# A train of 88 small matmuls at the head of TensorE's program, and all of group 0's first product in halves

## The chip, the cores and the metric

The kernel runs on one core of one Trainium2 chip. The metric is the device time of one launch in microseconds, the median of several executions. The profile is of one execution.

## What is computed

Two attentions over the same q, k and v (8 batches, 8 heads, 576 positions, 64 columns) are added, and the sum, laid out as 4608 tokens of 512 columns, goes through two matrix products with a gated activation between them. Cut to what matters:

```python
q_d, k_d, v_d = (t.reshape(B, H, S // 4, 4, D).mean(axis=3) for t in (q, k, v))
out_up = np.repeat(softmax(scale * q_d @ k_d.T) @ v_d, 4, axis=2)
scores = np.where(np.abs(pos[:, None] - pos[None, :]) < 4, scale * q @ k.T, -1e9)
x = (out_up + softmax(scores) @ v).transpose(0, 2, 1, 3).reshape(B * S, H * D)
h = x @ w_in                      # 4608x512 @ 512x2048
out = (h / (1 + np.exp(-1.702 * h))) @ w_out   # 4608x2048 @ 2048x512
```

## The kernel before

The tokens are cut into 9 groups of 512 (`TG`). For each group the first product (`mm1`, issued by `hps_mm`, L814) makes sixteen 128x512 accumulators, one for each chunk `ffc` of 128 hidden columns, each a sum over four chunks `dmc` of 128 model columns. ScalarE takes each through Silu into `gT` (L825). The second product (`mm2`, L892) multiplies `gT` by `w_out`. While group g is multiplied, the attention of batch g+1 is worked into the same TensorE program at hand-written positions (`POS`, `POS_0`), so that its output `xT` is there for the groups that follow.

The order on every engine is written by hand; nothing is scheduled. TensorE's program begins (L952 and on) with `warm(2)`: two matmuls of zeros in fp32, 128x128 by 128x512, each of which the hardware runs as two passes. They read `wz`, which VectorE's first instruction sets to zero (L126). Then come `bars0` (L411: the diagonal band of the score mask, from `id128` and `off`), a filler matmul of zeros (L959 in the profile), the scores of batch 0 (`scores0`, L423, which need `kT` and `qT`, the transposes of the first loads of k and q, L311), another `warm` on `PM[0]`, the coarse scores (`scores_d`, L466), the products with v (`av_local0`, L520; `av_down0`, L533), the pooled v (`prep_vd_pe`, L388), and four calls of `turned` (L575), which transpose the normalised result `y` (L557, VectorE) into PSUM; copies on ScalarE and VectorE (L586, L587) bring it to `xT`. Between the last `turned` calls stand the first parts of group 0's first product (`part`).

GpSimd issues the loads of k, q, v for batch 1 and of the weights, in one queue (q0 on the page): q and k of batch 0, v of batch 0, `w_in` in three parts (L281), k and q of batch 1 (L218), `w_out` in two parts (L290), the ten half chunks of v for batch 1 (`load_vb`, L249), and `w_out`'s other two parts. `prep_vd_pe(1, ...)` reads all five chunks of v for batch 1; it stands at place 36 of group 0 (`VDP_0`).

`hps_mm` issues one 512 column matmul, or two of 256 columns where `halved` holds. Before, that is in group 0 for `ffc` under 9 and `dmc` over 0, and in group 1 for `ffc` under 8 and `dmc` over 0. Each matmul in the program is a weight load (LDWEIGHTS, rows PEld) and a MATMUL (rows PE), so each halving adds two instructions to TensorE's program and no arithmetic.

Of the kernel before, what the change touches and what calls it, by code (L numbers as in the profile page):

```python
# [15 lines left out]
TG = 512  # L16
# [3 lines left out]
def kernel(  # L20
# [9 lines left out]
    nc = tc.nc  # L30
# [5 lines left out]
    n_dmc = d_model // 128  # L36
# [31 lines left out]
    for _ in range(2):  # L68
        t = work.tile([128, 2 * (S + SD)], FP32, name="l", tag="l", bufs=2).bitcast(BF16)
# [9 lines left out]
    def pm_tile():  # L79
        turn["m"] += 1  # L80
        return PM[turn["m"] % 2]

    wz = consts.tile([128, 512], BF16, name="wz")
# [92 lines left out]
    def make_up():  # L176
        nc.scalar.copy(out=up, in_=id128[:, :, None].to_broadcast([128, 128, 4]))
# [111 lines left out]
    def load_w_out(c):  # L289
        nc.gpsimd.dma_start(  # L290
            out=w_out_bf[:, 4 * c : 4 * c + 4, :],
            in_=bass.AP(
                tensor=moe_w_out.tensor, offset=moe_w_out.offset + c * 512 * d_model,
                ap=[[d_model, 128], [128 * d_model, 4], [1, d_model]],
            ),
        )
# [135 lines left out]
    def scores_mixed(b, qd, P):  # L432
        def local(i, a, half):
            for r in range(4):
                par = half if r < 2 else 1 - half
                rows = slice(32 * r, 32 * r + 32)
                k0 = 114 * i + KSTART[par]
                q0 = 114 * i + QSTART[par]
                nc.tensor.matmul(  # L439
                    P[1 + r // 2][64 * par : 64 * par + 64, r % 2, 60 * i : 60 * i + 60],  # L440
                    lhsT=kT[b, qd][rows, k0 : k0 + 64, a],
                    rhs=qT[b, qd][rows, q0 : q0 + 60, a],
                    start=(a == 0), stop=(a == 1),
                    tile_position=(32 * r, 64 * par),
                )

        if qd:
            for n in range(10):
                local(n // 2, n % 2, 0)
        for n in range(6):  # L450
            scores_d(b, qd, P[0], (n,))
            for a in range(2 if n < 5 else 0):
                local(n, a, 1)
        if not qd:
            for n in range(10):
                local(n // 2, n % 2, 0)
        return P[0], P[1:3]
# [17 lines left out]
    def exp_local(qd, sp, us=(0, 1)):  # L475
        for u in us:
            nc.scalar.activation(  # L477
                out=es[2 * qd + u][:, :, 0:300], in_=sp[u][:, :, 0:300],
                func=AF.Exp, scale=inv_sqrt_d,
            )  # L480
# [21 lines left out]
    def exp_down(qd, sd):  # L502
        nc.scalar.activation(  # L503
            out=eds[qd][:, :, 0:432], in_=sd[:, :, 0:432],
            func=AF.Exp, scale=inv_sqrt_d / 16.0,
        )

    def mask_local(qd):
        for u in range(2):
            ev = es[2 * qd + u][:, :, 0:300]  # L510
            nc.vector.tensor_tensor(out=ev, in0=ev, in1=mask, op=ALU.mult)  # L511
# [77 lines left out]
    def sub(t, off, *dims):  # L589
        return bass.AP(  # L590
            tensor=t.tensor, offset=t.offset + off,
            ap=[list(t.ap[0])] + [list(d) for d in dims],
        )
# [181 lines left out]
    def warm(n, t=None):  # L775
        t = pm_tile() if t is None else t
        for _ in range(n):
            nc.tensor.matmul(
                sub(t, 0, (256, 2), (1, 256)), lhsT=wzf[:, 0:128],
                rhs=wzf[:, None, :].to_broadcast([128, 2, 256]),  # L780
                start=True, stop=True,
            )

    def attention(b):
        st = {}

        def s_pe(qd):
            P = PB if b == 1 else PA
            st["d", qd], st["s", qd] = scores_mixed(b, qd, P)

        def s_act(qd):
            if qd == 0:
                nc.scalar.preload_act_table_set("natural_log_exp_and_others")
            if qd:
                exp_down(qd, st["d", qd])
            exp_local(qd, st["s", qd], (1, 0) if qd else (0, 1))
            if not qd:
                exp_down(qd, st["d", qd])
            mask_local(qd)

        def s1():
            s_pe(1)
            s_act(1)

        first = [lambda: s_pe(0), lambda: s_act(0), s1]
        if b == 1:
            return first + [lambda hp=hp: avx1(b, hp) for hp in range(HP)]
        return first + [lambda: avx(b, (0, 1)), lambda: avx(b, (2, 3))]

    def hps_mm(g, ffc, dmc, acc):  # L810
        halved = dmc and (ffc < 9 if g == 0 else g == 1 and ffc < 8)
        n = TG // 2 if halved else TG
        for c in range(0, TG, n):
            nc.tensor.matmul(  # L814
                acc[:, c : c + n],
                lhsT=w_in_bf[:, dmc, ffc * 128 : (ffc + 1) * 128],
                rhs=xT[dmc][:, g * TG + c : g * TG + c + n],
                start=(dmc == 0), stop=(dmc == n_dmc - 1 and c + n == TG),
            )

    def new_gT():
# [7 lines left out]
    def mm1(g, gT, steps):  # L829
        two = [PA[i][:, u, :] for i in range(3) for u in range(2)]  # L830
        bank, abreast = [PM[0], two[0], PM[1], two[2], two[4]], 4
        if g == 0:
            bank = acc[0:6] + late
        elif g == 1:
            bank, abreast = [two[0], two[2], two[1], two[3], PM[1]], 5
            bank = bank + [PM[0], two[4], two[0], two[2]] + PM[::-1] * 4
        else:
            bank = bank + bank + PM + PM + PM
        for ffc in range(n_ffc):
            for f in steps.get(ffc, ()):  # L840
                f()
            if g and ffc < abreast:
                if ffc == 0:
                    for dmcs in ((0, 1), (2,), (3,)):
                        for u in range(abreast):
                            for dmc in dmcs:
                                hps_mm(g, u, dmc, bank[u])
            elif g or ffc > 5:
                for dmc in range(n_dmc):
                    hps_mm(g, ffc, dmc, bank[ffc])  # L850
            else:
                continue
            silu(gT, ffc, bank[ffc])
# [94 lines left out]
    for qd in range(NQ):  # L948
        load_qk(1, qd)
    load_w_out(0)  # L950
    load_w_out(1)
    warm(2)  # L952
    make_up()
    make_psel0()
    prep_1("k", 0, 0)
# [5 lines left out]
        rhs=wzf[:, None, 0:196].to_broadcast([128, 2, 196]),  # L961
        start=False, stop=True, skip_group_check=True,
# [62 lines left out]
    def part(ffcs, *dmcs):  # L1025
        for dmc in dmcs:
            for ffc in ffcs:
                hps_mm(0, ffc, dmc, acc[ffc])
# [13 lines left out]
    for g in range(n_groups):  # L1042
# [36 lines left out]
        if b < B:  # L1079
            for n, f in zip(POS if g else POS_0, attention(b)):  # L1080
                steps.setdefault(n, []).append(f)
            if g == 0:
                steps.setdefault(VDP_0, []).append(lambda: prep_vd_pe(1, flat(PB[2])))
# [33 lines left out]
```

## Time and profile before

| | |
|---|---|
| median of 3 runs (lowest, highest) | 313.28 us (313.2, 314.6) |
| the profiled execution's own time | 313.27 us |
| its span, first to last instruction | 311.5 us |
| TensorE: matmul rows | 303.0 us busy, 4175 |
| TensorE: weight load rows | 157.4 us busy, 4175 |
| ScalarE, VectorE, GpSimd | 203.6, 147.6, 147.0 us busy |

The profiled execution's time is 1.8 us over its span, which is what lies around the first and the last instruction. Rows named PE are matmuls, PEld weight loads; a row of the timeline has start, length, engine, line, operation, what is written and read, the shape, a count, and in brackets the engine's idle time before it with what ended it ("issue" where the profile shows nothing that it waited for). Instruction loads have DMA queues of their own on the page (q8, q14).

### The profile page before, as it was taken

The page shows a single profiled execution, that of the slowest core. Times are in us where ns is not written, and L with a number is a line of the kernel's source. Part 1 is how long each engine was busy: PE and PEld are TensorE (multiplying, and loading weights), DVE is VectorE, ACT ScalarE, POOL GpSimd, SP SyncE. Part 2 cuts the span into 40 slices and gives each one's busy share as a digit, 9 for nine tenths or more (in the row PEclk, how much of TensorE's full clock was granted, in tenths as well). Part 3 has the DMA queues.
Part 4 walks back from the last instruction along what each step waited for, and adds up shares of the span by engine and source line. Part 5 has one row for each costly group of instructions (what it writes and reads, how often), then busy time and mean ns, then how long its engine had stood idle before and what let it go on. Part 6 is the DMA issues. An engine that isn't in the chain of part 4 may idle for free.

```text
span 311.5 us, 9625 instructions
## 1 busy us (share of the span) xinstructions
PE 303.0 (97%) x4175; PEld 157.4 (51%) x4175; DVE 147.6 (47%) x303; ACT 203.6 (65%) x325; POOL 147.0 (47%) x169
## 2 busy tenths in 40 slices
PE   7889999999999999999999999999999999999995
PEld 3557554664544554455545554555454544444444
DVE  5974937851594059605970399028902760000000
ACT  4746766787857786668866895689558857216611
POOL 8632294297039933795369634983396110000000
PEclk9999999999999999999999999999999999999999
DMA  6999999989727941695169705981520110010011
GB/s 103 162 211 207 170 105 210 229 236 184 192 99 162 216 124 69 170 230 145 69 165 204 176 36 175 194 189 58 151 75 33 39 67 2 34 67 36 0 67 67
DMA packets 64042, 39.94 MB, mean 128 GB/s; under 512 B 44544, under 2 KB 54912, under 8 KB 64000
## 3 DMA queue, kind: packets, MB, share of 16 engines
q0 software_dynamic: 18784, 14.95, 33.7%
q1 hardware_dynamic: 45072, 24.32, 28.4%
q8 instruction: 32, 0.52, 0.7%
q14 instruction: 10, 0.08, 0.1%
q10 hardware_dynamic: 144, 0.07, 0.1%
HBM read 44.83 MB, written 9.44 MB: 174 GB/s over the span
## 4 chain that ended last, share of the span: by engine, by line
PE 93%; DVE 2%; DMA 2%; issue 1%; ACT 1%; POOL 0%; DVEq 0%; ACTq 0%; POOLq 0%
PE pm L892 37%; PE pm L814 25%; PE pa L814 16%; PE pa L439 3%; PE pa L892 2%; PE pa L701 2%; PE pa L679 2%; PE pa L466 2%; DMA qb<-in_q_dram 2%; PE pm L909 1%; PE pa L575 1%; DVE qT L311 1%; PE pa L616 1%; PE pa L604 0%; PE pa L520 0%
## 5 line engine op out<-in xcount | busy, mean ns | idle before, releaser
L892 PE MATMUL pm<-w_out_bf,gT 128*128 128x512 bf16 x528 | 119.4, 379 | 0.0
L814 PEld LDWEIGHTS <-w_in_bf 128*128 128x128 bf16 x627 | 60.8, 98 | 61.5 <-issue 0.3
L814 PE MATMUL pm<-xT,w_in_bf 128*128 128x512 bf16 (+1 forms) x364 | 88.5, 372 | 0.0
L892 PEld LDWEIGHTS <-gT 128*128 128x128 bf16 x560 | 52.8, 98 | 62.4 <-issue 0.6
L825 ACT ACTIVATE gT<-pm 128x512 bf16<-128x512 f32 x88 | 52.8, 604 | 38.8 <-PE pm L814 38.8
L814 PE MATMUL pa<-xT,w_in_bf 128*128 128x512 bf16 (+1 forms) x263 | 59.0, 347 | 0.0
L511 DVE TENSOR_TENSOR es<-es,mask 128x600 bf16<-128x600 bf16 x28 | 17.3, 653 | 86.0 <-ACT es L477 85.8
L877 ACT ACTIVATE osb<-pm 128x512 f32<-128x512 f32 (+2 forms) x35 | 20.3, 582 | 30.5 <-PE pm L892 28.0
L825 ACT ACTIVATE gT<-pa 128x512 bf16<-128x512 f32 x56 | 31.8, 609 | 7.7 <-PE pa L814 7.7
L771 POOL TENSOR_TENSOR xT<-xT,od 128x576 bf16<-128x576 bf16 x12 | 15.4, 1282 | 43.7 <-DVE xT L755 43.7
L755 DVE TENSOR_TENSOR xT<-n,l 128x285 bf16<-128x285 f32 (+1 forms) x96 | 28.1, 363 | 0.0
L342 POOL TENSOR_TENSOR pq<-kT 128x576 f32<-128x576 bf16 x11 | 12.8, 1159 | 30.4 <-DVE kT L311 30.4
L879 DVE TENSOR_SCALAR osb<-pm 128x128 f32<-128x128 f32 x1 | 0.3, 292 | 53.8 <-ACT osb L877 53.8
L359 POOL TENSOR_TENSOR pq<-v 112x512 f32<-112x512 f32 x18 | 23.7, 1319 | 0.0
L311 DVE STREAM_TRANSPOSE kT<-kb 128x576 f32<-128x576 f32 x16 | 19.9, 1244 | 4.8 <-DMA kb<-in_k_dram 4.8
L311 DVE STREAM_TRANSPOSE qT<-qb 128x576 f32<-128x576 f32 x16 | 19.8, 1237 | 0.4 <-DMA qb<-in_q_dram 0.2
L503 ACT ACTIVATE ed<-pa 128x864 bf16<-128x864 f32 x16 | 14.3, 894 | 7.3 <-PE pa L466 7.3
L477 ACT ACTIVATE es<-pa 128x600 bf16<-128x600 f32 x28 | 17.2, 669 | 0.1
L750 ACT ACTIVATE l<-l 128x1440 f32<-128x1440 f32 x12 | 16.8, 1404 | 0.4
L745 DVE COPY n<-pa 128x492 f32<-128x492 f32 x24 | 15.0, 665 | 2.3 <-ACT l L744 1.7
L744 ACT ACTIVATE l<-pa 128x492 f32<-128x492 f32 x24 | 12.6, 578 | 4.2 <-PE pa L701 3.3
L439 PE MATMUL pa<-qT,kT 32*64 32x60 bf16 x1120 | 15.3, 195 | 0.0
(133 smaller groups left out, 352.9 us busy)
## 6 DMA issues: line engine op xcount, KB each, us to landing
out_dram<-osb SPq DMA_DIRECT2D x34, 256.0 KB, 2.1
vf<-in_v_dram SPq DMA_DIRECT2D x60, 128.0 KB, 4.6
v<-in_v_dram SPq DMA_DIRECT2D x72, 96.0 KB, 2.7
kb<-in_k_dram POOLq DMA_DIRECT2D x16, 288.0 KB, 6.4
qb<-in_q_dram POOLq DMA_DIRECT2D x16, 288.0 KB, 8.8
w_out_bf<-in_moe_w_out_dram POOLq DMA_DIRECT2D x4, 512.0 KB, 13.8
w_in_bf<-in_moe_w_in_dram POOLq DMA_DIRECT2D x2, 512.0 KB, 8.5
w_in_bf<-in_moe_w_in_dram POOLq DMA_DIRECT2D x1, 1024.0 KB, 13.6
```

The source lines that it names most:

```text
L311: nc.vector.transpose(out=t32.rearrange("p (i c) -> p c i", c=18), in_=store[b, qd].bitcast(FP32).rearrange("p (c d) -> p c d", c=18),)
L359: eng.tensor_tensor(out=t1[0:112], in0=x[:, :, 0:2, :], in1=x[:, :, 2:4, :], op=ALU.add)
L439: nc.tensor.matmul(P[1 + r // 2][64 * par : 64 * par + 64, r % 2, 60 * i : 60 * i + 60], lhsT=kT[b, qd][rows, k0 : k0 + 64, a], rhs=qT[b, ...
L477: nc.scalar.activation(out=es[2 * qd + u][:, :, 0:300], in_=sp[u][:, :, 0:300], func=AF.Exp, scale=inv_sqrt_d,)
L511: nc.vector.tensor_tensor(out=ev, in0=ev, in1=mask, op=ALU.mult)
L750: nc.scalar.activation(out=l, in_=l, func=AF.Exp, scale=-1.0)
L755: nc.vector.tensor_tensor(out=out, in0=sub(n, *part), in1=sub(l, *part), op=ALU.mult)
L771: eng.tensor_tensor(out=xs, in0=xs, in1=sub(od[:, u, :], 0, (1, SD), (0, 4)), op=ALU.add)
L814: nc.tensor.matmul(acc[:, c : c + n], lhsT=w_in_bf[:, dmc, ffc * 128 : (ffc + 1) * 128], rhs=xT[dmc][:, g * TG + c : g * TG + c + n], star ...
L825: nc.scalar.activation(out=gT[:, ffc, :], in_=acc, func=AF.Silu, scale=GELU_SCALE)
L877: eng.activation(out=osb, in_=ap, func=AF.Copy, scale=1.0 / GELU_SCALE)
L892: nc.tensor.matmul(ops[t], lhsT=gT[:, ffc, t * 128 : (t + 1) * 128], rhs=w_out_bf[:, ffc, :], start=(ffc == 0), stop=(ffc == n_ffc - 1),)
```

## The change

The first of the two `warm` matmuls gives way to 88 matmuls of zeros, 64x64 by 64x64, all on one corner of the array and into one PSUM tile. In group 0 every one of the 64 matmuls of the first product is now two halves; in group 1 one more `ffc` is halved. The start and stop flags follow: the first half starts the bank, and in group 0 every matmul has the stop flag. No arithmetic of the result is added or removed.

```diff
+    def small(n):
+        t = pm_tile()
+        for _ in range(n):
+            nc.tensor.matmul(
+                t[0:64, 0:64], lhsT=wz[0:64, 0:64], rhs=wz[0:64, 0:64],
+                start=True, stop=True, tile_position=(0, 0),
+            )
+
     def hps_mm(g, ffc, dmc, acc):
-        halved = dmc and (ffc < 9 if g == 0 else g == 1 and ffc < 8)
+        halved = g == 0 or (dmc and g == 1 and ffc < 9)
         n = TG // 2 if halved else TG
         for c in range(0, TG, n):
             nc.tensor.matmul(
                 acc[:, c : c + n],
                 lhsT=w_in_bf[:, dmc, ffc * 128 : (ffc + 1) * 128],
                 rhs=xT[dmc][:, g * TG + c : g * TG + c + n],
-                start=(dmc == 0), stop=(dmc == n_dmc - 1 and c + n == TG),
+                start=(dmc == 0 and c == 0), stop=(g == 0 or dmc == n_dmc - 1 and c + n == TG),
+                skip_group_check=(g == 0),
             )
@@
     load_w_out(0)
     load_w_out(1)
-    warm(2)
+    small(88)
+    warm(1)
     make_up()
     make_psel0()
```

## The prediction

> **What bounds the kernel.** I read the page's busy times first, then TensorE's waits, then the timeline around the one wait without a cause.
>
> ```profile
> PE 303.0 (97%) x4175; PEld 157.4 (51%) x4175; DVE 147.6 (47%) x303; ACT 203.6 (65%) x325; POOL 147.0 (47%) x169
> ...
> q8 instruction: 32, 0.52, 0.7%
> ...
> PE 93%; DVE 2%; DMA 2%; issue 1%; ACT 1%; POOL 0%; DVEq 0%; ACTq 0%; POOLq 0%
> ```
>
> TensorE sets the end. From 24.2 us on (the last `turned`) its matmuls stand end to end, with about 0.1 us at each change between full and small tiles and one 0.24. So a gain or loss before 24.2 us reaches the end unless a wait behind it takes it up. TensorE's waits in total:
>
> ```profile
> PE pa L423 <- DVE qT L311: 1.4, 1, 1.4
> ...
> PE pa L575 <- issue: 0.8, 1, 0.8
> ```
>
> The first line is slack: before the scores TensorE waits 1.4 us for qT, whose load lands at 7.0 us. The second stands inside the first `turned`:
>
> ```profile
> 18.49 0.27 PE L575 MATMUL pa<-id,y 128*128 128x117 bf16 x2
> 19.55 0.21 PE L575 MATMUL pa<-id,y 128*128 128x114 bf16 x1 [0.80 <-issue]
> ```
>
> Matmuls of one `turned` need nothing new, yet the next starts 1.01 us after the one before it (18.54), where its sisters follow in 0.05. Counted through the trace it is TensorE's instruction 449. On q8 the trace has 32 packets of 16,384 bytes; 4175 x 2 instructions against 32 packets is one packet per some 256. Packet starts follow that count: where long matmuls had run for a while they come 8 to 17 instructions ahead of numbers 193 + 256k, and where short ones run, up to 142 behind. So I read 0.8 as instruction 449 waiting for its program block, asked for when the block from 193 on is entered. Instruction 193 ran at 13.0; its packet ran from 16.29 to 18.14; 449 ran at 19.55: **6.55 us from entering a block to having the next one**. The second packet began 3.7 us after 449 and took only 0.97, so I bound it at 5.7 to 7.2. [...]
>
> **Part 1, the blocks.** One `warm` matmul is two matmul rows, so 4 instructions; 88 small ones are 176: +172 from there on. Group 0's product has 27 halved matmuls before and 64 after (+37, so +74 instructions, of which +12 for `ffc` 0 to 5), group 1 has 24 and 27 (+6). In total +252, four short of one block: from group 1 on the blocks change where they did, 4 instructions later. Only the front changes. New 193, 449, 705 are old 21 (in `bars0`), 277 (the first `av_local0`, L520, 14.71 us) and 533 (the second `turned`, 21.38 us, so 20.43 without the stall); the next change falls into the long matmuls of group 0 near 33 us, over 12 us behind. Old 449 is in the middle of a block: **-0.95** (the 1.01 us less an ordinary start).
>
> But the new second block must be there when old 533 comes. Old 277 waits for ScalarE's exponentials (they free its PSUM at about 14.6), so the block is entered at 14.68 and ready at 14.68 + 6.55 = 21.23, where TensorE wants it at 20.43: **+0.8**, bounds 0 (5.7 us of delay) to +1.5 (7.2). I take the same delay as before because the DMA engines are as busy around 18 us as around 16.3. TensorE has no slack there: its next wait, for y (22.13), ends as its own matmuls do (22.27).
>
> **Part 2, the train.** The first warm matmul goes: before, 1.19 to 4.77 held four passes, of which the last three are 0.853 apart. Row L778 at 9.00 has the same pass at 0.427 (1.12 for two with the drain), so the array runs at half rate until about 5.35 us, though the page's PEclk row shows 9 throughout. The two `bars0` rows show the step: 120 columns every 0.100 us at 4.77, every 0.05 at 11.4.
>
> ```profile
> 4.77 0.40 PE L411 MATMUL pa<-off,id 128*128 128x120 bf16 x2
> ...
> 5.17 1.06 PE L411 MATMUL pa<-off,id 128*128 128x480 bf16 x4
> ...
> 46.46 0.33 PE L616 MATMUL pa<-es,vb 64*64 64x60 bf16 x10
> ```
>
> The 64x64 by 64 train has no row of its own. Nearest is L616: 64x64 weights with 60 columns follow each other on one tile every 0.031 us (two tiles in turn, one start in 0.016), so 0.062 at half rate. Lower bound: columns alone, 64 / 120 x 0.100 = 0.053. Upper bound: the weight load not hidden, twice that, 0.107. With cadence c at half rate from 1.19 and c/2 from 5.35, the train ends at 5.35 + (88 - 4.16/c) x c/2 = 3.27 + 44c. Behind it: the second warm matmul 0.853 (full rate by then), `bars0` 4 x 0.05 + 4 x 0.203, the filler 0.655, 0.2 of drain: 2.71. Scores start at 5.98 + 44c against 8.325 before, so the delay is 44c - 2.345: **+0.38** at 0.062, 0.0 at 0.053, +2.36 at 0.107. The wait of 1.4 us is what hides the train, and it is used up. A delay passes on: exponentials, `scores_d`, ScalarE's next exponentials and old 277 follow each other with at most 0.06 of slack (L466 ends at 12.34, ScalarE goes on at 12.39).
>
> [...]
>
> **Part 3, the halves.** Two matmuls of 256 columns start 0.218 apart in sum (L814 from 24.6 on), one of 512 in 0.2155: 40 x 0.0025 = **+0.1**, on the path. The flags add no instruction or wait.
>
> **Part 4, what would be late next.** If the front gains, group 0's attention comes sooner, and the loads do not: GpSimd's queue is full from 12 us on. `prep_vd_pe(1)` starts at 44.19 and its last chunk of v, the last of the ten loads, is used at 44.89. It was issued at 40.25 and took 4.3 us, the longest of the two loads issued from 39.6 on:
>
> ```profile
> DMA to landing us min/median/max: 3.5/3.9/4.3
> ```
>
> It lands at 44.55, so TensorE can be there at most **0.34** sooner, whatever the front gains. `w_out`'s third part lands at 47.98 and is used at 49.7: not reached.
>
> **Sum.** +0.38 - 0.95 + 0.80 + 0.10 = +0.33, with a floor of -0.34. On the profiled execution's 313.27 (0.01 under the median): **313.6 us**.
>
> **Rivals.**
>
> *The stall only moves, and the train fits* (forecast, 0.55). By the bounds 312.9 (no new stall, train at 0.053, floor reached) to 314.3 (new stall 1.5, train at 0.062 and the rest as above).
>
> *The stall goes* (0.16). The new second block arrives by 20.43: +0.38 - 0.95 + 0.10 = -0.47, and v's landing cuts it to -0.34: 312.9. For it: the packet at 23.26 took half as long as the one at 16.29.
>
> *The wait at 449 is no block* (0.04). [...] Against it: all 32 packets follow the count.
>
> *The train costs more than the slack* (0.22, slower). Two ways with one price list. If weight loads on one tile are not hidden (0.10), cadence 0.107: +2.36 - 0.95 + 0.8 + 0.1 = +2.3, 315.6. If the quarter of the array doesn't raise the rate (0.12), the train takes 88 x 0.062 = 5.46 at half rate, the warm matmul 1.71, and `bars0` with the filler at half rate most of 3.3: scores start near 11.5, +3.2, and with the other terms +3.1, 316.4. It decides from c of about 0.08 us on. Against the first: L616 and L520 (65 columns behind 128 of weights every 0.031) both hide them. Against the second: from 13 to 18 us only small shapes run, with gaps, and the `turned` at 18.3 still is at full rate (345 columns in 0.158); but that is keeping the rate, not raising it.
>
> *Faster by over 0.5%* (0.03): it needs 1.57 us, more than all of the stall, and v would have to land earlier too.
>
> **Chances.** 0.5% is 1.57 us, about what a measurement of this kernel tells from no change. Within: 0.55 + 0.16 + 0.04 = 0.75. Slower: 0.22. Faster: 0.03. The range takes in the first three cases and the unhidden weight loads: 312.8 to 315.6.
>
> **What would show it.** TensorE's rows become 4175 + 126 = 4301. The L575 gap of 1.01 us is gone from the first `turned`; an "issue" gap of up to 1.5 us stands in the second one, at the old 533. The train's starts are 0.06 apart, then 0.03, and scores begin at 8.4 to 9.0. A q8 packet starts about 18 us, and one near 8. If instead TensorE waits at L388 near 44 us for v, the stall went away and the floor holds. Scores after 10 us would say that the train is the cost; a gap at the old place would say that blocks are not the cause.

## The result and the profile after

| | before | after |
|---|---|---|
| median (lowest, highest), 6 runs each | 313.24 us (312.93, 315.0) | 317.69 us (315.27, 318.37) |
| the profiled execution's own time | 313.27 us | 316.75 us |
| its span | 311.5 us | 315.0 us |
| TensorE: matmul rows, weight load rows | 4175, 4175 | 4301, 4301 |

The ratio is 1.0116, with a 95% interval of 1.0073 to 1.0159. The change makes the kernel slower by about 1.2%, 3.5 us in the profiled executions. The forecast of 313.6 us and its range (312.8 to 315.6) are both missed. The profiled execution's 316.75 us lies near the rival "the quarter of the array doesn't raise the rate" (316.4); the median is 1.3 above it. In some executions every kernel is a few us slower (before's own times beside the experiments run from 312.24 to 318.46 us), so single executions below are read by their traces, place by place.

The head of the page of after: TensorE's busy time rose by 4.0 us for 126 more rows, and q8 has one packet more.

```profile
span 315.0 us, 9877 instructions
...
PE 307.0 (97%) x4301; PEld 165.3 (52%) x4301; DVE 147.9 (47%) x303; ACT 203.5 (65%) x325; POOL 148.8 (47%) x169
...
q8 instruction: 33, 0.54, 0.7%
...
PE 95%; ACT 2%; issue 1%; DVE 1%; DVEq 0%; ACTq 0%
```

TensorE's waits of after (line, releaser, us in total, times, longest). The "issue" wait at L575 is gone, and two others are there, at lines which had none:

```profile
PE pm L901 <- issue: 1.3, 1, 1.3
...
PE pa L388 <- issue: 0.7, 1, 0.7
```

The timeline of after at its head:

```profile
1.19 4.90 PE L787 MATMUL pm<-wz 64*64 64x64 bf16 x88 [1.19 <-DVE wz L126]
6.02 2.07 PE L778 MATMUL pm<-wz 128*128 128x512 f32 x2
7.89 0.41 PE L411 MATMUL pa<-off,id 128*128 128x120 bf16 x2
...
10.67 0.23 PE L423 MATMUL pa<-qT,kT 32*128 32x120 bf16 x2
```

The two passes of the warm matmul take 2.07 us, where the row at 9.00 us of before had 1.12. The two matmuls of 120 columns at 7.89 take 0.41 together, as in the row of before at 4.77. So the array is at half rate until after 8 us. The trace's clock records agree: they have the rise from half to full at 9.93 us, and at 5.34 before. The scores start at 10.67 instead of 8.32.

The timeline of after where the first `turned` starts. The third matmul of the second row is the one that stood alone at 19.55 with 0.80 of idle time; it now follows the second by 0.05:

```profile
20.33 0.32 PE L575 MATMUL pa<-up,y 128*128 128x345 bf16 x1 [0.31 <-DVE y L557]
20.49 0.32 PE L575 MATMUL pa<-id,y 128*128 128x117 bf16 x3
20.64 0.24 PE L575 MATMUL pa<-up,y 128*128 128x167 bf16 x1
```

And the timeline of after at the two new waits, in group 0's second product and in the pooling of v for batch 1:

```profile
39.49 0.82 PE L901 MATMUL pm<-w_out_bf,gT 128*128 128x512 bf16 x3
41.59 0.38 PE L901 MATMUL pm<-w_out_bf,gT 128*128 128x512 bf16 x1 [1.28 <-issue]
...
46.71 0.64 PE L388 MATMUL pa<-vb,psel 128*64 128x256 bf16 x7
48.05 0.41 PE L388 MATMUL pa<-vb,psel 128*64 128x256 bf16 x4 [0.71 <-issue]
```

Counted through the trace (from 0, with the sequencer's own rows) the two waits stand at TensorE's instructions 1217 and 1473, which are 193 + 4 x 256 and 193 + 5 x 256 exactly. From one matmul's start to the next it is 1.66 and 0.98 us.

Where the 3.5 us come from is read by setting the same matmul of both traces side by side (times are starts):

| place | before | after | later by | step |
|---|---|---|---|---|
| first scores, L423 | 8.32 | 10.67 | 2.34 | the head |
| fourth matmul of the first `turned` | 19.55 | 20.59 | 1.04 | 0.97 of it the old wait, gone |
| scores in group 0, before 1217 | 37.44 | 38.55 | 1.11 | halves, +0.07 |
| instruction 1217, L901 | 39.04 | 41.59 | 2.55 | a new wait, +1.44 |
| instruction 1473, L388 | 44.56 | 48.05 | 3.50 | a new wait, +0.95 |
| last matmul | 307.62 | 311.14 | 3.52 | nothing more |

The theory after the result: the head costs 2 us because 64x64 matmuls don't raise the array's rate (in after it rises at 9.93 us, 8.7 us after the train's start), and the halves cost 2.4 us because they bring TensorE through a whole program block in less time than the next one takes to come (ahead of 1217, 3.87 us for the block and 5.53 until the next one is there). The rivals to it: the train costs by its mere length; the halves are harmless and the two waits follow from the late front; the old wait, once gone, leaves a gain that something else takes away.

### The profile page after: what moved, and what is told of

It reads as the page before. It is cut to its first block, busy times and chain, and to the rows that moved or that the text cites. A ratio compares the mean times of both kernels' runs of the same rounds, so it can differ in the third digit from the quotient of the medians.

```text
span 315.0 us, 9877 instructions
## 1 busy us (share of the span) xinstructions
PE 307.0 (97%) x4301; PEld 165.3 (52%) x4301; DVE 147.9 (47%) x303; ACT 203.5 (65%) x325; POOL 148.8 (47%) x169
## 4 chain that ended last, share of the span: by engine, by line
PE 95%; ACT 2%; issue 1%; DVE 1%; DVEq 0%; ACTq 0%
PE pm L901 37%; PE pm L822 24%; PE pa L822 15%; PE pa L439 3%; PE pa L901 2%; PE pa L701 2%; PE pa L466 2%; PE pa L679 2%; PE pm L787 2%; PE pm L918 1%; ACT l L485 1%; PE pa L575 1%; PE pa L411 1%; PE pm L778 1%; PE pa L616 1%
## 5 line engine op out<-in xcount | busy, mean ns | idle before, releaser
L901 PE MATMUL pm<-w_out_bf,gT 128*128 128x512 bf16 x528 | 119.6, 379 | 1.3 <-issue 1.3
L822 PEld LDWEIGHTS <-w_in_bf 128*128 128x128 bf16 x667 | 64.6, 98 | 58.1 <-issue 0.2
L901 PEld LDWEIGHTS <-gT 128*128 128x128 bf16 x560 | 52.7, 98 | 63.9 <-issue 2.1
L771 POOL TENSOR_TENSOR xT<-xT,od 128x576 bf16<-128x576 bf16 x12 | 17.2, 1434 | 41.5 <-DVE xT L755 41.1
```

What stands on the lines that cost most here:

```text
L771: eng.tensor_tensor(out=xs, in0=xs, in1=sub(od[:, u, :], 0, (1, SD), (0, 4)), op=ALU.add)
L822: nc.tensor.matmul(acc[:, c : c + n], lhsT=w_in_bf[:, dmc, ffc * 128 : (ffc + 1) * 128], rhs=xT[dmc][:, g * TG + c : g * TG + c + n], star ...
L901: nc.tensor.matmul(ops[t], lhsT=gT[:, ffc, t * 128 : (t + 1) * 128], rhs=w_out_bf[:, ffc, :], start=(ffc == 0), stop=(ffc == n_ffc - 1),)
```

## The experiments

In the expectations and below, a stall "at 449" is a wait of TensorE at its instruction 449, for the program block that begins there. That TensorE's program comes in blocks of 256 instructions is my reading of the traces: in after q8 has 33 packets of 16,384 bytes for 2 x 4301 instructions, one per some 260, and its two waits without a shown cause are 256 instructions apart.

### The train on the whole array, the train alone, the halves alone

`full_array_train` is the kernel after with the same 88 matmuls on 128x128 weights:

```diff
-                t[0:64, 0:64], lhsT=wz[0:64, 0:64], rhs=wz[0:64, 0:64],
-                start=True, stop=True, tile_position=(0, 0),
+                t[:, 0:64], lhsT=wz[:, 0:128], rhs=wz[:, 0:64],
+                start=True, stop=True,
```

> The changed kernel with one edit: the 88 zero matmuls use the whole array (128x128 weights, 64 columns) and not a quarter of it; count, columns and program blocks stay. Theory A (a quarter of the array does not raise the array's rate, and a block of 256 instructions that runs in under about 5.5 us stalls TensorE): the rate rises near 5.4 us as in the kernel before, scores start at 8.4 to 8.8 (10.67 in the changed kernel), the stalls at instructions 1217 and 1473 stay (about 1.5 and 0.9): 314.5 to 315.3 us, some 2 under the changed kernel. Rival B (small matmuls never raise the rate, whatever part of the array they use): as the changed kernel, 316.7 to 318. Rival C (the loss after 38 us is an echo of the late front): both later gaps go with the train's delay, 312.5 to 313.3.

Measured: 315.5 us (10 runs, 314.46 to 317.57), ratio 1.0043 (1.0003 to 1.0084). The timeline at the head:

```profile
1.20 4.80 PE L787 MATMUL pm<-wz 128*128 128x64 bf16 x88 [1.20 <-DVE wz L126]
5.83 1.10 PE L778 MATMUL pm<-wz 128*128 128x512 f32 x2
6.77 0.27 PE L411 MATMUL pa<-off,id 128*128 128x120 bf16 x2
...
8.55 0.23 PE L423 MATMUL pa<-qT,kT 32*128 32x120 bf16 x2
```

The train takes as long as in after (4.80 against 4.90 us), but what follows it runs twice as fast: 1.10 us for the warm matmul instead of 2.07, and the scores start at 8.55, 0.23 later than before. So the length of the train is not its cost; the rate behind it is. The time is just above the 314.5 to 315.3 us expected. The gain of 2.1 us at the scores does not reach the end, though: only the wait at 1473 is gone, and the one at 1217 has grown. The timeline there:

```profile
38.08 0.82 PE L901 MATMUL pm<-w_out_bf,gT 128*128 128x512 bf16 x2
41.14 0.38 PE L901 MATMUL pm<-w_out_bf,gT 128*128 128x512 bf16 x1 [2.24 <-issue]
```

TensorE stands 0.30 us ahead of before at 38.2 us and 2.10 behind it after this wait. It comes at the same instruction, with a front that is early. The two new waits do not follow from a late front.

`train_alone` is before with the new head (the train and one warm matmul), and groups 0 and 1 halved as before:

```diff
-    warm(2)
+    small(88)
+    warm(1)
```

> The kernel before with the train alone: 88 quarter-array matmuls and one warm, the halves as before. Theory A: the front as in the changed kernel (scores at 10.7, no gap in the first turned), then every block change lies 172 instructions earlier in the work, where bursts of short matmuls run a block in 3 to 5 us: a stall near the end of the scores in group 0 (about 1.6) and about two in each of the six groups with full attention (about 2.2 and 1.6): +24 us, 333 to 343 us. Rival C (only the train's own delay counts, blocks do nothing): +2.0 to +2.4, 315.3 to 315.7.

Measured: 318.5 us (one run), far below the 333 to 343 us expected. The head is that of after (rate up at 9.79 us), and the expected stalls in groups 1 and on are far smaller than I had worked out. Its waits for no shown cause in the small matmuls:

```profile
PE pa L616 <- issue: 1.2, 1, 1.2
...
PE pa L701 <- issue: 1.2, 3, 0.6
```

What failed is the delay: I had used one figure for the whole kernel, some 5.5 us from entering a block to having the next. Here it is 6.6 us for the block entered at 42.5 and 4.0 for the one entered at 80.1, and the three waits at L701 are 0.6 us at most. Why the delay varies is taken up below.

`halves_alone` is the other half of the change: `warm(2)` stays, and the first product is halved as in after.

```diff
-    small(88)
-    warm(1)
+    warm(2)
```

> The kernel before with the halves alone: both warm matmuls, no train. Theory A: the 0.8 issue wait in the first turned stays where it was (instruction 449), and from group 1 on block changes lie 80 instructions earlier in the work: a stall of about 1.6 near 41 us and one of about 2.2 in each of six groups: +14.6, 325 to 332 us. Rival C: +0.1, 313.4 us.

Measured: 325.06 us (one run). Its waits in TensorE:

```profile
PE pa L701 <- issue: 5.3, 6, 2.0
...
PE pa L575 <- issue: 1.1, 1, 1.1
```

The wait at L575 is still at 449, as block changes there were not moved. The six at L701 stand in six groups, at a block change among that group's small matmuls. The halves shift these by 80 instructions, out of step with the long ones; the 172 instructions of the train, added to them, make nearly a whole block of 256 and bring the changes back. So in these single executions the two parts, each worse alone (spans of 316.7 and 323.3 us), are better together (315.0). Neither alone has the wait of after at 1217 (0.19 us from start to start in `train_alone`, 0.39 here): it takes both shifts. The time also holds a stretch of another kind (columns: window, its length, busy time of PE, PEld, DVE, ACT, POOL, granted clock, DMA share, GB/s):

```profile
13.00:19.80 6.80, 5.44 (x137) 3.85 (x137) 5.76 (x8) 4.26 (x8) 4.31 (x7) 1.00 1.42 180
19.90:26.60 6.70, 6.51 (x64) 4.44 (x64) 3.61 (x9) 2.21 (x6) 1.46 (x2) 0.50 1.13 213
```

From 19.86 us, at the end of the wait at 449, the granted clock is 0.50 for 6.8 us, and again for 3.4 us from 88.12, behind the longest wait at L701 (2.04, up to 86.84). This one run does not show why; so its 325.06 is not a clean price of the halves. An estimate: half of the two stretches is 5.1 us, and the last matmul starts 11.8 us later than in before, so the halves alone would still cost some 6.7 us.

### Which part of the array raises the rate

Two kernels are after with another shape of the train, one with all columns and 64 rows of contraction, one with all rows and 64 columns of weights:

```diff
-                t[0:64, 0:64], lhsT=wz[0:64, 0:64], rhs=wz[0:64, 0:64],
+                t[:, 0:64], lhsT=wz[0:64, 0:128], rhs=wz[0:64, 0:64],      # train_64_rows
+                t[0:64, 0:64], lhsT=wz[:, 0:64], rhs=wz[:, 0:64],          # train_64_cols
```

> The changed kernel with the 88 zero matmuls on half the array, 64 rows by 128 columns of weights. What raises the rate is open: if rows do not matter, the rise comes at 5.3 to 6.7 us and scores start near 8.6; if it takes rows as well, the rise comes near 9.9 and scores start near 10.7 as with a quarter.

> The changed kernel with the 88 zero matmuls on the other half, 128 rows by 64 columns of weights. If columns do not matter, the rise comes at 5.3 to 6.7 us and scores start near 8.6; if it takes columns as well, near 9.9 and 10.7. If it is the share of the array that counts, this one and the one with 64 rows agree.

Measured: 317.57 and 315.63 us (one run each). The timeline at the head of `train_64_rows`, and then of `train_64_cols`:

```profile
1.20 4.87 PE L787 MATMUL pm<-wz 64*128 64x64 bf16 x88 [1.20 <-DVE wz L126]
6.00 2.07 PE L778 MATMUL pm<-wz 128*128 128x512 f32 x2
7.86 0.41 PE L411 MATMUL pa<-off,id 128*128 128x120 bf16 x2
```

```profile
1.19 4.58 PE L787 MATMUL pm<-wz 128*64 128x64 bf16 x88 [1.19 <-DVE wz L126]
5.70 1.12 PE L778 MATMUL pm<-wz 128*128 128x512 f32 x2
6.66 0.27 PE L411 MATMUL pa<-off,id 128*128 128x120 bf16 x2
```

Both use half of the array. With 64 rows the warm matmul behind the train takes 2.07 us, with 128 rows 1.12. The clock records put the rise at 11.09 and 5.17 us. So in these two it is not the share of the array: the train with 128 rows of contraction raises the rate, the one with 64 does not. `train_64_cols` is a second copy of `full_array_train` behind that, with one wait of 2.00 us at 1217; `train_64_rows` a second copy of after, with waits of 1.0 and 1.0 at 1217 and 1473.

The clock records say one thing more. The stretches between two changes of the clock are whole numbers of steps of 3.413 us (before has 90 of them, after 89, `halves_alone` 4, 2, 18, 1 and 68, `trim_8` 1, 2 and 87), and the steps lie elsewhere in each of these executions (one begins at 1.93 us in before, at 3.10 in after, at 4.26 in `train_64_rows`). In before, after, `train_64_rows`, `train_64_cols` and `quarters_late_use` the step that ends with the rise is the first that 128-row matmuls fill to 94% or more: it begins at 1.93, 6.52, 7.68, 1.76 and 0.99 us. The step before it in after (3.10 to 6.52) is as full of matmuls, but until 6.02 they are the train's, and it does not raise the rate. In `train_64_rows` the step from 4.26 to 7.68 has 128-row matmuls for 1.7 us and does not raise it either; the next one does, so its rise is at 11.09 and its scores start at 11.23, 0.56 later than in after. So between these two executions the cost of the head differs with the place of the steps.

The rise came 3.2 to 5.5 us after the first matmul of 128 rows in before (1.19 to 5.34), after (6.02 to 9.93), `quarter_warm` (4.80 to 8.40), `train_64_rows` (6.00 to 11.09), `train_64_cols` (1.19 to 5.17), `quarters_late_use` (1.19 to 4.40) and `quarters_early` (1.19 to 6.67). With 64 rows it is otherwise: in after and `train_64_rows` 4.8 us of them did not raise the rate.

`quarter_warm` asks what the late rise costs without the rest. It is before, with both warm matmuls on a quarter of the array:

```diff
+    def warm_q(n):
+        t = pm_tile()
+        for _ in range(n):
+            nc.tensor.matmul(
+                sub(t[0:64], 0, (256, 2), (1, 256)), lhsT=wzf[0:64, 0:64],
+                rhs=wzf[0:64, None, :].to_broadcast([64, 2, 256]),
+                start=True, stop=True, tile_position=(0, 0),
+            )
-    warm(2)
+    warm_q(2)
```

> The kernel before with its two first matmuls of zeros cut to a quarter of the array (64x64 weights, same fp32 passes, same 512 columns): as many instructions and as long, so no program block moves. Theory A (a quarter of the array does not raise the array's rate): the rate rises after 8.2 us and not at 5.3, bars0 starts near 4.8 and runs at half rate, scores start at 8.3 to 8.6, and the wait for qT at 12.9 takes most of it: 313.2 to 314.8 us with the 0.8 wait at instruction 449 still there. Rival B (any matmul raises it): rise at 5.3 to 6.7, 313.2 to 313.5.

Measured: 314.41 us (4 runs, 313.46 to 317.27), ratio 1.0023 (0.9955 to 1.009). The timeline at its head:

```profile
1.19 3.67 PE L787 MATMUL pm<-wz 64*64 64x512 f32 x4 [1.19 <-DVE wz L126]
...
5.17 1.81 PE L411 MATMUL pa<-off,id 128*128 128x480 bf16 x4
...
8.55 0.23 PE L423 MATMUL pa<-qT,kT 32*128 32x120 bf16 x2 [0.26 <-DVE qT L311]
```

`bars0` is at half rate (1.81 us against 1.06 before), the records have the rise at 8.40, and the scores still start at 8.55: the wait for qT hides all of it, with 0.26 us to spare. The wait at 449 is still there, but with 0.29 us of idle time and not the 0.8 expected. A late rise costs 2 us in after because the train also makes the head longer (`bars0` starts at 7.89 us there and at 4.80 here), and the wait is used up.

### Where the gain of the removed wait goes

`quarters_early` has the array warmed as before, and block changes at such places that no wait for a block should be left. It adds 43 small matmuls on the whole array behind `warm(2)`, and quarters in group 0:

```diff
-        halved = dmc and (ffc < 9 if g == 0 else g == 1 and ffc < 8)
-        n = TG // 2 if halved else TG
+        n = TG
+        if g == 0 and ffc < 9:
+            n = TG // 4
+        elif g == 1 and ffc < 8 and dmc:
+            n = TG // 2
...
     warm(2)
+    small(43)
```

> A version meant to beat both: two warm matmuls, then 43 full-array zero matmuls (full rate by then, inside the 1.4 us wait for qT), group 0's first nine chunks in quarters of 128 columns, the rest of group 0 whole, group 1 as before: +248 instructions, all of them before the long matmuls that precede the scores of batch 1. Theory A: no stall at instructions 449, 705, 961, 1217 or 1473, scores at 8.3, quarters cost about 0.2, and the landing of v for batch 1 near 44.5 us takes up what is gained beyond 0.34: 312.8 to 313.3 us. Rival C (blocks do nothing, the 0.8 stays): 313.4 to 313.6.

Measured: 313.58 us (12 runs, 313.18 to 316.88), ratio 1.0001 (0.9963 to 1.0039). No wait for a block is left in the trace, and nothing is gained. (Twenty gaps of 0.16 us in the long matmuls of the second product, at L904, are no waits: 41 matmul records are missing from this trace, and a weight load starts in the middle of such a gap.) The timeline of `quarters_early` has a new wait ahead of the place of the old one:

```profile
14.69 0.35 PE L520 MATMUL pa<-vb,l 128*128 128x65 bf16 x6
16.07 0.42 PE L388 MATMUL pm<-vb,psel 128*64 128x256 bf16 x4 [1.04 <-DMA vb<-in_v_dram]
```

TensorE waits for the fourth chunk of v of batch 0, which in before landed in time. It is 1.12 us behind before here, and 0.31 behind where the old wait of 0.97 ended. That chunk's load is issued at 7.2 us. The trace's answer for the issues of v there (smallest, median and largest time to landing; in before it holds the chunk ahead of it too), in before, after and `quarters_early`:

```profile
DMA to landing us min/median/max: 7.5/7.6/7.7
```

```profile
DMA to landing us min/median/max: 8.4/8.4/8.4
```

```profile
DMA to landing us min/median/max: 8.9/8.9/8.9
```

The cause that fits is the first q8 packet of 16,384 bytes, which is earlier when instructions are added ahead of it:

| kernel | first q8 packet | v's fourth chunk lands | last chunk lands |
|---|---|---|---|
| before | 16.29 to 18.14 | 14.83 | 15.67 |
| `trim_12` | 17.15 | 14.82 | |
| `quarter_warm` | 16.55 to 17.84 | 15.03 | |
| after | 9.10 to 10.08 | 15.56 | 16.43 |
| `full_array_train` | 9.12 to 10.09 | 15.44 | |
| `train_64_rows` | 9.67 to 10.65 | 15.88 | |
| `quarters_early` | 13.57 to 14.98 | 16.03 | 16.96 |
| `quarters_late_use` | 12.82 to 14.09 | 15.74 | |

Where the packet comes while v is on its way, v lands 0.6 to 1.2 us later; where it comes behind v, v lands within 0.25 us of before. The eight traces of the table agree. The other chunks say the same. In `quarters_early` the third lands only 0.29 later than in before (14.07 against 13.78) and the fourth 1.20 later; in `quarters_late_use` the third is not later (13.73) and the fourth is, by 0.91. In after, whose packet comes while the first chunk is on its way, the first already lands 0.81 later (12.49 against 11.68). But no run moved the packet and nothing else, so that the packet is the cause is argued from these rows.

`quarters_late_use` is `quarters_early` with the attention of batch 1 at later places in group 0, so that its v is needed later:

```diff
-    POS_0 = [16, 18, 28, 40, 49, 58, 67]
-    VDP_0 = 36
+    POS_0 = [16, 18, 28, 44, 52, 60, 68]
+    VDP_0 = 40
```

> The version with quarters (no program block stall, but it waited 1.0 us for v of batch 1 at 43.7) with the pooled v of batch 1 and the four calls behind it moved back by four, four, three, two and one matmuls. Theory A (what removing the stall gains is lost to the landing of v): the wait goes or falls under 0.2 and the time falls by 0.5 to 0.9, to 312.6 to 313.1 us. Rival D (the wait is not what cost it: the same time is lost behind it): 313.4 to 313.7, as without the move.

Measured: 313.74 us (6 runs, 313.48 to 316.27), ratio 0.9998 (0.9948 to 1.0048). No gain: my floor by v of batch 1 was not what held the time. The expectation has the wait of `quarters_early` at 43.7 us and at v of batch 1; it stands at 16.07 and is for v of batch 0. It is the same here, and the later places do not touch it:

```profile
PE pm L388 <- DMA vb<-in_v_dram: 0.8, 1, 0.8
```

`trim_12` and `trim_8` move the block changes the other way, by leaving out matmuls of zeros at the front: `trim_8` the filler behind `bars0` and `warm(1, t=PM[0])`, `trim_12` one of the two first warm matmuls as well.

```diff
-    warm(2)
+    warm(1)                      # trim_12 only
...
-    nc.tensor.matmul(
-        sub(PM[1], Q0, (196, 2), (1, 196)), lhsT=wzf[:, 0:128],
-        rhs=wzf[:, None, 0:196].to_broadcast([128, 2, 196]),
-        start=False, stop=True, skip_group_check=True,
-    )
...
-    warm(1, t=PM[0])
```

> The kernel before with three of its zero fillers left out (one of the two first warm matmuls, the filler of 392 columns before the scores, the warm matmul after them): 12 instructions fewer ahead of everything, so block changes come 12 instructions later in the work (old 205 and 461 in place of 193 and 449), the first block load still starts after v of batch 0 is down. Theory A: v of batch 0 lands as before (14.8 to 15.1 for its fourth chunk), the stall moves into the second group of L533 after the first turned and shrinks from 0.95 to 0.2 to 0.6, later blocks stay free of stalls: 312.6 to 313.1 us, unless the array, with less to do, runs the scores at half rate (then 313.3 to 315). Rival C (blocks do nothing): 313.3.

> As the kernel with 12 instructions fewer, with both first warm matmuls: 8 fewer, block changes at old 201 and 457. Theory A: a stall of 0.3 to 0.8 at old 457, the last matmul of the first turned; 312.7 to 313.2 us, or the same proviso on the array's rate after 8.4 us.

Measured: 313.77 us (12 runs, 313.41 to 317.71), ratio 0.9988 (0.9956 to 1.0019); and 313.63 us (10 runs, 312.77 to 316.81), ratio 0.9971 (0.993 to 1.0011). Both are the same as before within the interval. No wait of over 0.45 us at 449 is left in either, and a slower front stands in its place. `trim_8` by stretches (columns as in `halves_alone`):

```profile
3.00:9.40 6.40, 4.33 (x51) 2.04 (x50) 4.23 (x8) 2.67 (x8) 6.32 (x12) 1.00 1.03 171
9.50:16.20 6.70, 5.81 (x85) 3.34 (x85) 6.03 (x6) 4.74 (x9) 4.43 (x8) 0.50 1.97 160
16.40:24.00 7.60, 7.22 (x144) 5.02 (x144) 6.20 (x12) 3.56 (x9) 2.15 (x3) 1.00 1.18 208
```

Without the two fillers the array falls back to half rate from 9.5 to 16.2 us, and TensorE reaches the L388 row that before has at 14.96 at 16.36, 1.40 us later. In `trim_12` it is at half rate from the start: two passes of the warm matmul (1.19 to 3.27) and `bars0` (3.97 to 6.16) do not raise it, and the records have the rise at 16.63, behind a step that 128-row matmuls fill to about half, with 32-row ones among them; why that one raises the rate stays open. So in this front the matmuls of zeros raise the rate and hold it: in before, which has them all, the records have full rate from 5.34 us to behind the last matmul. The two edits don't show what the wait at 449 alone is worth, as the front behind which it vanished is slower. No kernel of these ten beats before by more than its interval.

### What the delay of a block is made of

With all traces the delay can be split. There are 19 waits of over 0.4 us from one start to the next that the profile puts down to nothing else and that are not missing records. Counted by the weight loads, of which none is missing, all 19 stand exactly at an instruction 193 + 256k. Nine of them:

| kernel, instruction | entered | packet starts after | packet takes | from its end to the next block | in total | wait, start to start |
|---|---|---|---|---|---|---|
| before, 449 | 13.01 | 3.28 | 1.84 | 1.42 | 6.54 | 1.01 |
| `quarter_warm`, 449 | 13.23 | 3.32 | 1.29 | 1.42 | 6.03 | 0.50 |
| after, 1217 | 36.06 | 2.40 | 1.55 | 1.58 | 5.53 | 1.66 |
| after, 1473 | 41.59 | 4.01 | 0.89 | 1.56 | 6.46 | 0.98 |
| `full_array_train`, 1217 | 34.66 | 3.28 | 1.61 | 1.60 | 6.49 | 2.62 |
| `train_64_cols`, 1217 | 34.87 | 2.77 | 1.82 | 1.66 | 6.25 | 2.38 |
| `train_64_rows`, 1473 | 41.87 | 4.34 | 0.89 | 1.49 | 6.73 | 1.24 |
| `train_alone`, 2497 | 80.05 | 1.75 | 0.96 | 1.34 | 4.04 | 0.80 |
| `halves_alone`, 3521 | 117.61 | 1.96 | 0.88 | 1.56 | 4.40 | 1.15 |

The last part is the same at all 19: **1.3 to 1.7 us from the packet's end to the next block**. And at the changes without such a wait the next block is never used sooner than that after its packet's end: 2.83 us or more in before, 2.03 or more in after. What varies is when the packet starts (0.9 to 4.3 us after the block is entered, at the 19 waits) and how long it takes (0.9 to 1.9); in total it is 3.7 to 6.9 us. It also says why `full_array_train` has no wait at 1473: there the packet started 1.7 us after the block was entered and was over at 44.02, and TensorE came 2.5 us later. And why its wait at 1217 grew: the block was entered 1.40 us sooner than in after, and its packet started only 0.53 sooner (37.93 against 38.46). What sets the packet's start is not settled.

Most changes show no such wait. After has 2 waits at 33 packets, behind blocks that ran in 3.87 and 5.49 us; its quickest block without one took 5.70 us, and the quickest of before 5.82.

## Why the prediction was wrong, step by step

**The failing steps are two:** in part 2, that a quarter of the array raises the rate, and in part 1, that the next changes are far from their limit.

*Part 2, the train: +0.38 forecast, +2.34 at the scores measured, +2.0 behind them.* The term was sized with the rise at 5.35 us, as behind the long matmul, and no run shows it: behind a train of 64 rows the rise came at 9.93 in after and at 11.09 in `train_64_rows`. The train itself I had nearly right: 88 matmuls at half rate take 4.83 us, 0.055 each, where I took 0.062 with 0.053 below. With a rise in time the same sum holds: `full_array_train` has its scores at 8.55, +0.23. The rival "the quarter of the array doesn't raise the rate" had the right mechanism and +3.2; it was too high, as the cadence was 0.055 and the rate did rise at 9.93, under the filler. I gave it 0.12, on the ground that small shapes hold the rate between 13 and 18 us; that ground was weak, since many of those matmuls (L388, L520, L411) have 128 rows. And it is not the quarter that matters, as I had put it, but the 64 rows. A slip beside it: by the forecast's own terms the train makes the kernel 1.57 us slower from a cadence of 0.09 us on (44 x 0.09 - 2.345 - 0.05), not about 0.08.

*Part 1, the old wait: -0.95 forecast, -0.97 measured.* Right, in the place that was named.

*Part 1, a new wait at old 533: +0.8 forecast, 0 measured.* The block was entered at 16.72, two us later than I had it, since the front was late, and its packet ran from 19.41 to 20.38; with the 1.3 to 1.7 us behind it the next block was there by 22.1, and TensorE came at 22.42. My delay of 6.55 us, taken from one block, was too long here by at least 0.85 us, as TensorE came after 5.70 and did not wait. With the front in time (`full_array_train`) there was no wait either. So "the stall goes" would have been right for this change alone.

*Part 1, behind it: 0 forecast, +1.44 and +0.95 measured.* I wrote that the next change falls into group 0's long matmuls, "over 12 us behind". That is the time from the change before it to this one. What had to be asked as well is how long TensorE takes through the block that this change opens. By the count the change falls at 34.9 us of before, not near 33, so the block opens only 2.5 us ahead of batch 1's scores (37.34). It holds the last of the new halves (`ffc` 13 to 15), and then some 208 instructions, nearly all of them small matmuls that run in about 1 us: 256 instructions in 3.87 us (36.06 to 39.93), where the next block took 5.53. The block behind that took 5.49 us (41.59 to 47.08), against 6.46. By my own 5.7 to 7.2 us I could have forecast both, from rows of before, which takes 4.2 us from 34.87 to 39.04 and 5.5 from there to 44.56. And "from group 1 on the blocks change where they did" was right, but inside group 0 they change elsewhere. It was luck that the profiled time came near one of my rivals: that rival had +3.2 for the head, where 2.0 reached the products with v, and nothing for these two waits.

*Part 3, the halves: +0.1 forecast.* +0.07 measured between 20 and 37 us, where most of them are. As arithmetic they cost little; their cost is the count of instructions.

*Part 4, the floor of v of batch 1: -0.34.* Not reached, and not the floor that mattered. In `quarters_early`, where the wait at 449 is gone and the array warm, v of batch 0 was late instead, some 28 us ahead of the place that I had named. I had asked what is late next after the gain, and only at the loads with the least time left; I had not asked what the packet, moved to an earlier time, does to the loads beside it.

The sum as measured: 2.34 (the head) - 0.33 (slack up to the products with v, so 2.01 there) - 0.97 + 0.07 + 1.44 + 0.95 = +3.50, against +3.52 at the last matmul. It is the sum of one execution of each kernel. The six times of after spread over 3.1 us, and in `train_64_rows`, its near copy, the two waits are 1.38 and 1.24 us from start to start where after has 1.66 and 0.98. So the sizes of the two waits, like the time of the rise, belong to this execution; their places do not.

## What to carry to other kernels

All 19 waits for a block stood here at instructions 193 + 256k, so an edit that adds instructions moves the changes that come later in the work of that engine. Go through each block that it moves, and compare the time that its 256 instructions run with the time until the next block is there (here 3.7 to 6.9 us where TensorE waited), for the block in front of a change and for the one behind it. Look too at what each block's own load now runs beside (here v landed 0.6 to 1.2 us later beside one). Warm the array with matmuls over all 128 rows (here the scores started at 8.44 and 8.55 us behind trains with 64 and 128 columns of weights, at 10.67 and 11.23 behind trains of 64 rows), and look at the clock records before taking zeros out of a light front: here they held the rate (`trim_8`, without two of them, was at 0.50 from 9.5 to 16.2 us).

## What the runs showed of the hardware that was not expected

- 88 matmuls of zeros with 64 rows of contraction, 4.8 us of them, did not raise the array's rate, whether they had 64 columns of weights or 128 (rise at 9.93 and 11.09 us); with 128 rows and 64 columns they did (5.17).
- The page's row of the granted clock shows 9 from the start in after, where the two passes at 6.02 us run at half rate: ahead of the first clock record, at 9.93 us, it does not show the rate.
- The clock's changes lie whole numbers of steps of 3.413 us apart (90 in before, 89 in after), and the steps lie elsewhere in each of the executions above. In five of them the rise ends the first step that 128-row matmuls fill to 94% or more (in after 6.52 to 9.93), in `trim_12` one that they fill to about half.
- The rate was lost again in a light stretch: `trim_8` is at 0.50 from 9.5 to 16.2 us, and TensorE's longest idle time ahead of it was 2.0 us.
- Where TensorE waits for a block, the block is there 1.3 to 1.7 us after the end of its packet, at all 19 waits. The packet takes 0.9 to 1.9 us and starts 0.9 to 4.3 us after the block is entered.
- Where the first packet came while v was on its way, v's fourth chunk landed 0.6 to 1.2 us later. That the packet does it is argued, not isolated. Open too: why the start of a packet varies, and why `halves_alone` ran 6.8 and 3.4 us at half rate behind two of its waits.
